# A three-stage kernel on one core: a plan of its own for the first two groups, loads of x ahead of their casts, a second output buffer

## The chip, the core and the metric

The kernel runs on one core of a Trainium2 chip. TensorE (PE) multiplies, VectorE (DVE) and ScalarE (ACT) work on its results, GpSimd (POOL) sets up constants, and the SyncE queue (SP) issues all DMAs. The metric is the device time of one execution, in microseconds; 0.2% is 2.1 us.

## The reference

```python
qn = q / (np.linalg.norm(q, axis=1, keepdims=True) + 1e-06)   # q, k, v: 1 x 6016 x 256
kn = k / (np.linalg.norm(k, axis=1, keepdims=True) + 1e-06)
s = kn.transpose(0, 2, 1) @ qn / tau                          # 256 x 256
a = softmax(s)                                                # rows, with + 1e-09 below
x = v @ a                                                     # 6016 x 256
x = relu(x @ w_in1) ** 2 @ w_out1                             # 256 -> 2048 -> 256
h = x @ w_in2
out = np.maximum(0.01 * h, h) @ w_out2                        # 256 -> 2048 -> 256
```

All in float32; the weights come as 64-bit floats and are turned into 32-bit ones on the chip.

## The kernel before, in words

**Prologue.** The 47 token tiles of q and k come in 14 groups of loads (1, 2, then ten of 4, then 3 and 1 tiles, `groups`). For each group PE adds q^T k into two PSUM banks (L425), ACT squares the group (`square`, L390 to L399), and DVE adds the square to one sum of four tiles (`accumulate`, L406). After the last group DVE folds the sum to one tile (L420 to L422), and eight matmul calls with a vector of ones (`norm_sums`, L373) give the norms. A call in float32 is two instructions in the trace. A chain of small steps follows: norms, scaled product, transposes, exponentials, transposes back (`eT`), and a first **fold** (L277): the attention matrix goes into the first weight block, so that x itself is never formed in the first pass. Between the steps stand matmuls on an identity (`keep_warm`).

**Two passes over units.** Each of the two expert layers is a pass of six panels of tokens by eight groups of 256 hidden columns: 96 units `n` in all, panel by panel. A float32 number is kept as a high and a low part, and every product is three matmuls (`mm3`, L566 to L568: low x high, high x high, high x low). Unit `n` has first products `h` (x with w_in) and second products `y` (g with w_out), the latter issued one or two units later. Units 0 to 7 (`plain`, L684) have four first products of six matmuls, four second products of six, and the fold for the next group; the others (`strassen`, L710) have seven first products of three matmuls. ACT applies relu (L691), square (L662) and the cast to g's high part (L655); DVE makes g's low part (L137). The first products of the plain units take three PSUM banks, a, b, e and a again, each to be freed by its relu.

**Conversions.** A weight block (`Unit`) is turned into high and low parts in some steps of DVE (L173 to L195), a rebias on ACT (L176), a cast on ACT (L222) and a low part on DVE (L137); `whl` is a block of w_in, `wo` one of w_out. For the first pass this runs between the plain units.

**x of later panels** (`prepare_x`). In the first pass v is loaded and transposed; in the second the first pass's result comes back from memory by one DMA into `xr` (L912). ACT casts it in four pieces (L932), DVE makes the lows and three sums.

**Output** (`y_done`, L613 to L627). A finished `y` is copied or transposed from PSUM into the tile `o`, of which there is one, and stored; the very last panel goes another way (`finish_last`, L638 and L639).

**What sets the order.** Nothing is scheduled by need. Each step has a time in a plan (`at`, `on`, `fit`; a unit of the plan is about one matmul of 512 columns), where `fit` looks for a gap in a list of what DVE or ACT already has (`Gaps`). All steps are sorted by these times, and each engine runs its instructions in that order. A plain unit has one table of offsets, stretched by 1.14 (`STRETCH`), 62 units long.

Of the kernel before, what the change touches and what calls it, by code (L numbers as in the profile page):

```python
# [8 lines left out]
F32 = mybir.dt.float32  # L9
# [8 lines left out]
P = 128  # L18
# [32 lines left out]
def attn_moe_moe2(  # L51
# [74 lines left out]

    ts, stt, tt = nc.vector.tensor_scalar, nc.vector.scalar_tensor_tensor, nc.vector.tensor_tensor
    order = tc.manual_schedule()
    order.__enter__()
# [181 lines left out]

    later = []

    def flush():
        while later:
            later.pop(0)()

    def converted(units):

        units[0].exponent()  # L320
        later.append(units[0].rebias)
        yield
        for i, u in enumerate(units):
            if i + 1 < len(units):
                units[i + 1].exponent()
                later.append(units[i + 1].rebias)
                yield
            for step in (u.mantissa, u.mantissa_low, u.sign, u.high):
                step()
                if step == u.high:  # L330
                    later.append(lambda: (u.round(), later.append(u.low)))
                yield
# [8 lines left out]
    with (  # L341
        tc.tile_pool(name="att", bufs=1) as att,
        tc.tile_pool(name="att4", bufs=AHEAD) as att4,
        tc.tile_pool(name="att2", bufs=2) as att2,
    ):
# [21 lines left out]
        steps_o = converted([first_o])  # L367
        W0 = 4

        def norm_sums(src, first):  # L370

            for b in range(4):
                nc.tensor.matmul(  # L373
                    pn[:, b : b + 1],
                    src[:, b * P : (b + 1) * P],
                    ones,
                    start=first and b == 0,
                    stop=not first,
                    skip_group_check=True,
                )  # L380


# [3 lines left out]
        def square(n, t):  # L386
            g = groups[n][1]
            flat = t.rearrange("p g a c -> p g (a c)")
            if n == whole[0]:
                nc.scalar.activation(acc, flat, AF.Square)  # L390
                return
            squares[n] = att2.tile([P, G, 2 * C], F32, tag="sq", name="sq")
            if n < NS - 1:
                nc.scalar.activation(squares[n][:, :g], flat[:, :g], AF.Square)
                return

            last = squares[n][:, 0]
            nc.scalar.activation(last[:, :C], flat[:, 0, :C], AF.Square)
            nc.scalar.activation(ordered(last[:, C:]), in_order(flat[:, 0, C:]), AF.Square)  # L399

        def accumulate(n):
            if n < whole[0]:
                return
            for i, at in ((0, 0), (1, 1)) if n == whole[0] else ((n, 0),):
                sq, g = squares.pop(i), groups[i][1]
                tt(acc[:, at : at + g], acc[:, at : at + g], sq[:, :g], op=ALU.add)  # L406

        for n, (t0, g) in enumerate(groups):
            t = qk.pop(n)
            last_group = n == NS - 1  # L410
            square(n, t)
            if last_group:
                nc.scalar.activation(small[:, 7, 0:1], ones, AF.Sqrt)
            flush()
            if n and not last_group:
                accumulate(n - 1)
            if last_group:
                accumulate(n - 1)
                a0, a1 = acc[:, 0], acc[:, 1]
                tt(acc[:, 0:2], acc[:, 0:2], acc[:, 2:4], op=ALU.add)  # L420
                tt(sums_[:, :C], a0[:, :C], a1[:, :C], op=ALU.add)
                tt(ordered(sums_[:, C:]), in_order(a0[:, C:]), in_order(a1[:, C:]), op=ALU.add)  # L422
# [12 lines left out]
            if W0 <= n < W0 + 4:  # L435
                run(steps_i, 2)
            elif W0 + 4 <= n < W0 + 6:
                run(steps_i, 1)
            if n + AHEAD < NS:
                load_qk(n + AHEAD)  # L440
            elif n + AHEAD == NS:
                load_v(0, 0)
                first_o.load()
                nc.sync.dma_start(tau_sb, tau.partition_broadcast(P))
                load_v(0, 1)
            if n == W0 + 7:
                for u in others[:2]:
                    u.load()
            if last_group:
                norm_sums(squares[n][:, 0], True)  # L450
                norm_sums(sums_, False)
        flush()
        run(steps_o, 2)
        later.pop(0)()
        nc.vector.reciprocal(rtau, tau_sb)
# [16 lines left out]
        run(steps_o, 1)  # L472
        flush()
        s = [bank("e", "s0"), bank("y3", "s1")]
# [30 lines left out]
        x_transpose(1, 0)  # L505
        x_high(0)
        for i in range(KC):
# [8 lines left out]
        for j in range(KC):  # L516
            split(*eT[j], pe[j][:, :C])
        x_high(3)
        x_transpose(0, 1)
# [3 lines left out]
        for i in range(KC):  # L523
            fold_high(i, *first_fold[i])
            fold_low(i, *first_fold[i])
        store_folded(0)
        x_transpose(1, 1)
        x_high(1)
        x_high(2)
        run(steps_o, 3)  # L530
        x_low(1)
        x_low(2)
        flush()
        flush()
        first_o.store()
# [7 lines left out]
    plan = []  # L543
    DVE, ACT = Gaps(), Gaps()

# [13 lines left out]
    LAST = 2 * NP * NG - 1  # L559
    STRETCH = 1.14  # L560
    units = {}
    g_t, c_t, s_t, y_t, h_t = {}, {}, {}, {}, {}

    def mm3(ps, a, b, first, last):
        (ah, al), (bh, bl) = a, b
# [32 lines left out]
    def y_done(t, n, half):  # L598
# [9 lines left out]
        def take(d):  # L608
            ys = y_t[key]
            if d == 0:  # L610
                o[0] = vpool.tile([P, 16, C // Q], F32, tag="o", name="o", bufs=1)
            if L == 2:
# [61 lines left out]
    def plain(n, t0):  # L674

        L, p, g = units[n]
        w = WIDTH[p]
        T = lambda x: t0 + STRETCH * x
        x_at = {(0, 0): (2, 0), (0, 1): (2, 1), (1, 1): (1, 0), (1, 0): (1, 1)}

        def first(half, fb, tag):
            h = h_t[n, half, fb] = bank(tag, "h")
            for kc in range(KC):
                which, at_ = x_at[kc, half]  # L684
                a, b = both(wi_t[L, p, g], 2 * kc + fb), both(x_t[(L, p), which], at_, slice(0, w))
                mm3(h[:, :w], a, b, kc == 0, kc == KC - 1)

# [5 lines left out]
        if g + 1 < NG:  # L693
            pw = {}
            at(T(24), lambda: pw.update(enumerate(fold(g + 1))))
            for i in range(KC):
                on(ACT, T(31 + 2.2 * i), 2.1, lambda i=i: fold_high(i, *pw[i]))
                on(DVE, T(37 + 2.6 * i), 2.5, lambda i=i: fold_low(i, *pw[i]))
            at(T(43), store_folded, g + 1)
        for x, half, fb, tag in ((0, 0, 0, "a"), (12, 0, 1, "b"), (30.4, 1, 0, "e"), (42.4, 1, 1, "a")):  # L700
            at(T(x), first, half, fb, tag)
            on(ACT, T(x + 6.4), 2.7, relu, half, fb)
        for half, x in ((0, 21.2), (1, 51.6)):
            on(ACT, T(x), 4.6, nonlinear, n, half, w, "square")
            on(ACT, T(x + 4.2), 4.6, nonlinear, n, half, w, "cast")
            on(DVE, T(x + 9), 5.4, nonlinear, n, half, w, "low")
        seconds(T, n, ((6, (2, 1, 1)), (18, (1, 0, 0)), (36.4, (1, 0, 1)), (48.4, (1, 1, 0))))

# [88 lines left out]
    for n in range(LAST + 1):  # L797
        L, p, g = units[n] = n // (NP * NG) + 1, n // NG % NP, n % NG
        lengths.append(54.4 * STRETCH if n < NG else 45 * (WIDTH[p] + 32) / 544)
        start.append(now)  # L800
# [56 lines left out]
    for i, u in enumerate(others):  # L857
        end = convert(u, 0, i < 2)
        due = start[u.g - 1] + 24 * STRETCH if u.kind == "i" else start[u.g + 1] + 18 * STRETCH
        assert end < due, (u.kind, u.g, end, due)  # L860
# [32 lines left out]
    def prepare_x(L, p):  # L893
# [108 lines left out]
```

## Time and profile before

| | us |
|---|---|
| median of 3 runs (1073.13 to 1074.63) | 1074.62 |
| the profiled execution | 1073.74 |
| its span, first to last instruction | 1072.0 |
| PE busy in it | 1043.0 |
| DVE busy | 788.6 |
| ACT busy | 716.7 |

The prologue takes the first 62 us of the span, the eight plain units go on to about 164 us, the second pass begins near 570 us. Busy times of engines overlap; what counts is where PE stands still or runs at the lower of its two clocks, and which engine it waits for there.

### The profile page before, as it was taken

What the parts mean: (1) busy time and instruction counts of PE and PEld (TensorE: products, weight loads), DVE (VectorE), ACT (ScalarE), POOL (GpSimd) and SP (SyncE); (2) the same over time, 40 slices, a digit from 0 to 9 for tenths busy, and PEclk for the clock granted to TensorE, in tenths of its full rate; (3) what the DMA queues carried; (4) which work ended last, traced back from release to release, by engine and by line L of the source; (5) the groups of instructions that cost most, each with busy time, mean ns of one, the idle gap of its engine ahead of it and who ended that gap; (6) DMA issues with size and microseconds to landing.
All of it is one profiled execution on the core that took longest, in us unless ns stands there. A gap on an engine that the chain in (4) does not pass through costs nothing.

```text
span 1072.0 us, 12819 instructions
## 1 busy us (share of the span) xinstructions
PE 1043.0 (97%) x4774; PEld 879.4 (82%) x4774; DVE 788.6 (74%) x1097; ACT 716.7 (67%) x851; POOL 0.7 (0%) x6
## 2 busy tenths in 40 slices
PE   8979999999999999999998999999999999999997
PEld 6758888888888788998886888888888888898886
DVE  3899956887988888888885756766766765766554
ACT  5568867888888887887885655655555555555543
POOL 0000000000000000000000000000000000000000
PEclk9989999999999999999998999999999999999999
DMA  9939338557658758656556435535544544645431
GB/s 331 267 136 260 136 99 189 188 223 201 226 210 260 231 195 272 220 222 253 217 211 235 161 119 201 168 142 190 161 160 176 167 162 158 191 162 174 160 119 40
DMA packets 118590, 203.48 MB, mean 190 GB/s; under 512 B 52608, under 2 KB 66176, under 8 KB 116864
## 3 DMA queue, kind: packets, MB, share of 16 engines
q1 hardware_dynamic: 118528, 202.66, 55.9%
q8 instruction: 38, 0.62, 0.2%
q14 instruction: 24, 0.20, 0.1%
HBM read 165.15 MB, written 37.49 MB: 189 GB/s over the span
## 4 chain that ended last, share of the span: by engine, by line
PE 87%; DMA 5%; DVE 4%; SPq 1%; ACT 1%; issue 1%; DVEq 0%
PE y L568 14%; PE y L566 14%; PE y L567 14%; PE hc L566 4%; PE hc L568 3%; PE hc L567 3%; PE ha L566 3%; PE ha L567 3%; PE ha L568 3%; PE hb L566 3%; PE hb L568 3%; PE hb L567 3%; PE sT L425 2%; DMA xr<-x 2%; PE y L586 2%; PE he L566 2%
## 5 line engine op out<-in xcount | busy, mean ns | idle before, releaser
L567 PE MATMUL y<-g,wo 128*128 128x512 f32 (+1 forms) x736 | 283.9, 386 | 0.0
L566 PE MATMUL y<-g,wo 128*128 128x512 f32 (+1 forms) x736 | 283.8, 386 | 0.0
L568 PE MATMUL y<-g,wo 128*128 128x512 f32 (+1 forms) x736 | 283.8, 386 | 0.0
L137 DVE TENSOR_TENSOR g<-c,g 128x1024 fp32r<-128x1024 f32 (+1 forms) x192 | 230.4, 1200 | 30.3 <-ACT g L655 24.5
L655 ACT CAST g<-c 128x1024 fp32r<-128x1024 f32 (+1 forms) x192 | 198.8, 1035 | 4.6
L664 ACT ACTIVATE c<-c 128x1024 f32<-128x1024 f32 (+1 forms) x96 | 100.3, 1045 | 139.4 <-DVE c L754 139.0
L567 PEld LDWEIGHTS y<-g,wo 128*128 128x128 f32 x736 | 138.5, 188 | 26.1
L568 PEld LDWEIGHTS y<-g,wo 128*128 128x128 f32 x736 | 138.5, 188 | 25.9
L566 PEld LDWEIGHTS y<-g,wo 128*128 128x128 f32 x736 | 138.5, 188 | 25.7
L660 ACT ACTIVATE c<-c 128x1024 f32<-128x1024 f32 (+1 forms) x80 | 83.2, 1040 | 41.4 <-DVE c L754 41.1
L754 DVE TENSOR_TENSOR c<-u,hc 128x512 f32<-128x512 f32 (+1 forms) x88 | 59.5, 676 | 58.6 <-PE hc L568 57.7
L662 ACT ACTIVATE c<-c 128x1024 f32<-128x1024 f32 (+1 forms) x96 | 100.4, 1045 | 1.8
L754 DVE TENSOR_TENSOR c<-c,hb 128x512 f32<-128x512 f32 (+1 forms) x88 | 59.3, 674 | 57.2 <-PE hb L568 51.9
L754 DVE TENSOR_TENSOR c<-w,hc 128x512 f32<-128x512 f32 (+1 forms) x88 | 59.2, 672 | 40.5 <-PE hc L568 39.8
L743 ACT COPY u<-ha 128x512 f32<-128x512 f32 (+1 forms) x88 | 50.9, 578 | 56.5 <-PE ha L568 54.1
L754 DVE TENSOR_TENSOR w<-u,he 128x512 f32<-128x512 f32 (+1 forms) x88 | 59.2, 673 | 33.2 <-PE he L568 31.2
L566 PE MATMUL hc<-x,wi 128*128 128x512 f32 (+1 forms) x176 | 69.1, 393 | 6.8 <-DVE c L754 6.8
L567 PE MATMUL ha<-x,wi 128*128 128x512 f32 (+1 forms) x176 | 68.1, 387 | 0.0
L566 PE MATMUL hb<-x,wi 128*128 128x512 f32 (+1 forms) x176 | 68.1, 387 | 0.0
L566 PE MATMUL ha<-x,wi 128*128 128x512 f32 (+1 forms) x176 | 68.1, 387 | 0.0
L567 PE MATMUL hc<-x,wi 128*128 128x512 f32 (+1 forms) x176 | 68.0, 387 | 0.0
L568 PE MATMUL hc<-x,wi 128*128 128x512 f32 (+1 forms) x176 | 68.0, 386 | 0.0
(122 smaller groups left out, 1515.2 us busy)
## 6 DMA issues: line engine op xcount, KB each, us to landing
wi<-wi SPq DMA_DIRECT2D x80, 896.0 KB, 4.9
wo<-wo SPq DMA_DIRECT2D x96, 512.0 KB, 5.6
wi<-wi SPq DMA_DIRECT2D x24, 512.0 KB, 3.6
wst<-in_moe_w_in_dram SPq DMA_DIRECT2D x16, 512.0 KB, 5.6
wst<-in_moe_w_out_dram SPq DMA_DIRECT2D x16, 512.0 KB, 4.4
wi<-wis SPq DMA_DIRECT2D x8, 1024.0 KB, 4.8
qk<-in_q_dram SPq DMA_DIRECT2D x10, 512.0 KB, 8.2
qk<-in_k_dram SPq DMA_DIRECT2D x10, 512.0 KB, 8.3
```

The source lines that it names most:

```text
L137: tt(lo, x, raw(hi), op=ALU.subtract)
L425: nc.tensor.matmul(sT[j][:, :C], t[:, i, 0, j * P : (j + 1) * P], t[:, i, 1], start=n == 0 and i == g - 1, stop=last_group and i == 0,)
L566: nc.tensor.matmul(ps, al, bh, start=first, stop=False, skip_group_check=True)
L567: nc.tensor.matmul(ps, ah, bh, start=False, stop=False, skip_group_check=True)
L568: nc.tensor.matmul(ps, ah, bl, start=False, stop=last, skip_group_check=True)
L586: nc.tensor.matmul(ys[t // 2][:, t % 2 * C : (t % 2 + 1) * C], gt[:, a, fb, t * P : (t + 1) * P], wo[:, b, :, fb], start=first and m == 0 ...
L655: nc.scalar.copy(g_t[n, half][:, 0, :, :w], c)
L660: nc.scalar.activation(c, c, AF.Relu)
L662: nc.scalar.activation(c, c, AF.Square)
L664: nc.scalar.activation(c, c, AF.Prelu, alpha=0.01)
L743: nc.scalar.copy(to, h_t[n, tag][:, :w])
L754: tt(to, x, h_t[n, tag][:, :w], op=ALU.add)
```

## The change

- *Norms.* DVE sums only the ten groups of four; the squares of the last two groups (3 tiles and 1) go straight to the norm products, which are 16 calls instead of 8. There are three square buffers instead of two. Conversions start one group later, and a pending step of ACT now comes ahead of the group's square, one of DVE behind its accumulation.
- *After the exponentials* one cast of x moves behind the casts of `eT`, and both highs of the first folded block come ahead of both lows.
- *Plain units.* Units 0, 1 and the rest have a table each (`PLAIN`), 36, 50 and 62 units long; unit 1 has its four first products in a row, ahead of the fold and of unit 0's second products. The first products take banks a, b, e in turn over all units. Their three matmuls are high x high, high x low, low x high.
- *x in the second pass.* The load keeps its time in the plan; the first step on it comes 66 units later instead of 22.
- *Output.* In the second pass `o` takes its buffer from the pool of v's tiles, which has two.

```diff
-            if n < NS - 1:
+            if n <= whole[-1]:
                 nc.scalar.activation(squares[n][:, :g], flat[:, :g], AF.Square)
                 return
...
+            nc.scalar.activation(squares[n][:, :g, :C], flat[:, :g, :C], AF.Square)
+            for i in range(g):
+                nc.scalar.activation(ordered(squares[n][:, i, C:]), in_order(flat[:, i, C:]), AF.Square)
...
-            if last_group:
-                norm_sums(squares[n][:, 0], True)
-                norm_sums(sums_, False)
+        for i in range(3):
+            norm_sums(squares[NS - 2][:, i], first=i == 0)
+        norm_sums(sums_)
+        norm_sums(squares[NS - 1][:, 0], last=True)
...
+    PLAIN = [
+        dict(first=(0, 6, 18.4, 24.4), fold=12, second=(), length=36, relu=(6.4, 12.4, 26.9, 34.2), stretch=1,
+             square=(18, 36.9), cast=(29.6, 44.4), low=(34.7, 49.5), fold_high=22.6, fold_low=27),
...
-        nc.tensor.matmul(ps, al, bh, start=first, stop=False, skip_group_check=True)
-        nc.tensor.matmul(ps, ah, bh, start=False, stop=False, skip_group_check=True)
-        nc.tensor.matmul(ps, ah, bl, start=False, stop=last, skip_group_check=True)
+    def mm3(ps, a, b, first, last, terms=((1, 0), (0, 0), (0, 1))):
+        for i, (m, n) in enumerate(terms):
+            nc.tensor.matmul(ps, a[m], b[n], start=first and i == 0, stop=last and i == 2, skip_group_check=True)
...
+                o[0] = vpool.tile([P, 16, C // Q], F32, name="o", **({"tag": "v"} if L == 2 else {"tag": "o", "bufs": 1}))
...
-        ot = vpool.tile([P, G, C], F32, tag="o", name="o", bufs=1)
+        ot = vpool.tile([P, G, C], F32, tag="v", name="o")
...
-            begin += LOAD
+            begin += 3 * LOAD
```

On PE, from unit 1's first products on, before (`h` first products, `y` second products, `pw` the fold):

```order
L566 MATMUL h<-x_402,wi 128x512
L567 MATMUL h<-x_402,wi 128x512
L568 MATMUL h<-x_402,wi 128x512
L566 MATMUL h<-x_403,wi 128x512
L567 MATMUL h<-x_403,wi 128x512
L568 MATMUL h<-x_403,wi 128x512
L566 MATMUL y_640<-g,wo 128x512
L567 MATMUL y_640<-g,wo 128x512
L568 MATMUL y_640<-g,wo 128x512
L566 MATMUL y_641<-g,wo 128x512
L567 MATMUL y_641<-g,wo 128x512
L568 MATMUL y_641<-g,wo 128x512
```

And now:

```order
L574 MATMUL h<-x_416,wi 128x512 x3
L574 MATMUL h<-x_417,wi 128x512 x3
L574 MATMUL h<-x_416,wi 128x512 x3
L574 MATMUL h<-x_417,wi 128x512 x3
L574 MATMUL h<-x_416,wi 128x512 x3
L574 MATMUL h<-x_417,wi 128x512 x3
L574 MATMUL h<-x_416,wi 128x512 x3
L574 MATMUL h<-x_417,wi 128x512 x3
L278 MATMUL pw<-whl,eT 128x256 x12
L574 MATMUL y_662<-g,wo 128x512 x3
L574 MATMUL y_663<-g,wo 128x512 x3
L574 MATMUL y_662<-g,wo 128x512 x3
```

Before, a second product of unit 0 stands after two first products of unit 1 (the second of them is shown); now unit 1's four first products and the fold stand ahead of three second products, the first and half of the second of which are shown.

On ACT, from the first relu (`c<-h`) on, before:

```order
L691 ACTIVATE c<-h 128x512
L222 CAST whl<-cm 128x512
L176 ACTIVATE ce<-ce,rebias 128x512
L691 ACTIVATE c<-h 128x512
L662 ACTIVATE c<-c 128x1024
L655 CAST g<-c 128x1024
L295 ACTIVATE wi<-pw,rs 128x256 x2
L691 ACTIVATE c<-h 128x512
L222 CAST wo<-cm 128x512
L176 ACTIVATE ce<-ce,rebias 128x512
L691 ACTIVATE c<-h 128x512
L662 ACTIVATE c<-c 128x1024
```

And now:

```order
L700 ACTIVATE c<-h 128x512 x2
L223 CAST whl<-cm 128x512
L669 ACTIVATE c<-c 128x1024
L296 ACTIVATE wi<-pw,rs 128x256 x2
L700 ACTIVATE c<-h 128x512
L662 CAST g<-c 128x1024
L700 ACTIVATE c<-h 128x512
L669 ACTIVATE c<-c 128x1024
L700 ACTIVATE c<-h 128x512
L662 CAST g<-c 128x1024
L700 ACTIVATE c<-h 128x512
L669 ACTIVATE c<-c 128x1024
```

Of the four conversion steps (the casts of `whl` and `wo`, two rebiases `ce`) that stood between the first four relus, the cast of `whl` is left; the highs of the fold (`wi<-pw`) come ahead of the first cast to `g`, which now stands behind the third relu.

On ACT, where the second panel of the second pass is prepared (`x<-xr` the casts of the loaded panel), before:

```order
L662 ACTIVATE c<-c 128x1024
L655 CAST g<-c 128x1024
L743 COPY u<-ha 128x512
L222 CAST wos<-cm 128x512
L932 CAST x_4925<-xr 128x512
L664 ACTIVATE c<-c 128x1024
L655 CAST g<-c 128x1024
L618 COPY o<-y_4305 128x512
L664 ACTIVATE c<-c 128x1024
```

And now:

```order
L752 COPY u<-ha 128x512
L223 CAST wis<-wr 128x1024
L223 CAST wos<-cm 128x512
L671 ACTIVATE c<-c 128x1024
L662 CAST g<-c 128x1024
L625 COPY o<-y_4319 128x512
L671 ACTIVATE c<-c 128x1024
L752 COPY c<-ha 128x512
L662 CAST g<-c 128x1024
L625 COPY o<-y_4357 128x512
L752 COPY u<-ha 128x512
L943 CAST x_5023<-xr 128x512
```

The first cast of the loaded panel, of 512 columns, has moved from ahead of the leaky relu (the ACTIVATE `c<-c` after it) to behind the next group's copy of `u`, one unit later.

## Rows read from the trace of the kernel before

**Rows 1.** The page's first part: busy us, share of the span, instructions.
```profile
PE 1043.0 (97%) x4774; PEld 879.4 (82%) x4774; DVE 788.6 (74%) x1097; ACT 716.7 (67%) x851; POOL 0.7 (0%) x6
```

**Rows 2.** Busy time by stretch: length, engines' busy us, PE's granted clock, DMA.
```profile
core 0: us, PE busy (x) PEld busy (x) DVE busy (x) ACT busy (x) POOL busy (x), PEclk, DMA share, GB/s
10.10:48.20 38.10, 38.10 (x176) 33.29 (x176) 28.66 (x23) 22.89 (x15) 0.00 (x0) 1.00 1.13 331
...
50.40:57.10 6.70, 5.17 (x23) 4.87 (x24) 4.93 (x15) 2.97 (x6) 0.00 (x0) 0.50 0.19 69
...
70.80:76.90 6.10, 0.00 (x0) 0.00 (x0) 5.96 (x11) 6.04 (x11) 0.00 (x0) 0.78 0.65 218
...
84.00:94.00 10.00, 10.00 (x48) 8.38 (x48) 9.86 (x18) 8.54 (x13) 0.00 (x0) 1.00 1.20 281
...
576.00:582.80 6.80, 5.58 (x13) 4.41 (x14) 3.59 (x5) 3.45 (x5) 0.00 (x0) 0.50 0.26 84
```

**Rows 3.** Timeline of PE from 48 to 95: start, us, instruction, idle before.
```profile
48.77 1.05 PE L373 MATMUL pn<-ones,sq 128*128 128x1 f32 x8 [0.48 <-ACT sq L398]
...
51.90 1.87 PE L373 MATMUL pn<-ones,sums 128*128 128x1 f32 x8 [2.08 <-DVE sums L421]
...
59.57 1.89 PE L277 MATMUL pw<-whl,eT 128*128 128x256 f32 x12
...
62.75 0.50 PE L566 MATMUL h<-x,wi 128*128 128x512 f32 x1 [1.29 <-DVE wi L298]
...
77.00 0.79 PE L566 MATMUL h<-x,wi 128*128 128x512 f32 x1 [6.26 <-ACT c L691]
...
90.02 0.39 PE L566 MATMUL h<-x,wi 128*128 128x512 f32 x1
...
94.10 0.39 PE L566 MATMUL y<-g,wo 128*128 128x512 f32 x1
```

**Rows 4.** Groups of instructions, 62 to 104: busy us, mean ns, idle before.
```profile
L691 ACT ACTIVATE c<-h 128x512 f32<-128x512 f32 x13 | 7.7, 595 | 3.4 <-PE h L568 3.4
L195 DVE SCALAR_TENSOR_TENSOR cm<-cm,ce 128x512 f32<-128x512 f32 x10 | 6.9, 692 | 0.3
L662 ACT ACTIVATE c<-c 128x1024 f32<-128x1024 f32 x6 | 6.4, 1062 | 0.2
L137 DVE TENSOR_TENSOR g<-c,g 128x1024 fp32r<-128x1024 f32 x5 | 6.1, 1218 | 0.0
...
L295 ACT ACTIVATE wi<-pw,rs 128x256 fp32r<-128x256 f32 x7 | 3.0, 474 | 0.8 <-DVE wi L298 0.8
```

**Rows 5.** The chain that ended last, in order of time: start, us, what.
```profile
80.78 0.42 PE h L568
81.20 0.23 PE h L566
...
482.40 7.39 DMA xr<-x
...
566.17 9.03 DMA xr<-x
```

**Rows 6.** Timeline of PE at the four later waits.
```profile
491.81 0.50 PE L566 MATMUL hc<-x,wi 128*128 128x512 f32 x1 [1.01 <-DVE c L754]
...
577.22 0.79 PE L566 MATMUL hc<-x,wi 128*128 128x512 f32 x1 [3.76 <-DVE c L754]
...
836.53 0.50 PE L566 MATMUL hc<-x,wi 128*128 128x512 f32 x1 [0.45 <-DVE c L754]
...
918.37 0.47 PE L566 MATMUL hc<-x,wi 128*128 128x448 f32 x1 [1.05 <-DVE c L754]
```

**Rows 7.** Timeline of the end, all engines.
```profile
1061.46 3.03 PE L586 MATMUL y<-wo,g 128*128 128x256 f32 x24
...
1067.01 0.76 DVE L638 COPY o<-y 128x256 f32<-128x256 f32 x2 [4.63 <-DMA out_dram<-o]
...
1068.20 0.40 SPq L639 DMA_DIRECT2D out_dram<-o  x1
```

More of the change, by code (lines that the diff above doesn't have):

```diff
@@ L127, in attn_moe_moe2 @@
     ts, stt, tt = nc.vector.tensor_scalar, nc.vector.scalar_tensor_tensor, nc.vector.tensor_tensor
+    DVE, ACT = Gaps(), Gaps()
     order = tc.manual_schedule()
@@ L310, in x_tile, with flush @@
         return x_t[key, which]
[L312 to L316, printed above, removed]
+    later = {ACT: [], DVE: []}
+    def flush(engine):
+        steps, later[engine] = later[engine], []
+        for step in steps:
+            step()
     def converted(units):
         units[0].exponent()
-        later.append(units[0].rebias)
+        later[ACT].append(units[0].rebias)
         yield
@@ L325, in converted @@
                 units[i + 1].exponent()
-                later.append(units[i + 1].rebias)
+                later[ACT].append(units[i + 1].rebias)
                 yield
@@ L330, in converted @@
                 if step == u.high:
-                    later.append(lambda: (u.round(), later.append(u.low)))
+                    later[ACT].append(u.round)
+                    later[ACT].append(lambda u=u: later[DVE].append(u.low))
                 yield
@@ L367, in attn_moe_moe2, with norm_sums @@
         steps_o = converted([first_o])
-        W0 = 4
-        def norm_sums(src, first):
+        W0 = 5
+        def norm_sums(src, first=False, last=False):
             for b in range(4):
+                x = src[:, b * P : (b + 1) * P]
                 nc.tensor.matmul(
[L374 to L379, printed above, removed]
+                    pn[:, b : b + 1], x, ones, start=first and b == 0, stop=last, skip_group_check=True
                 )
@@ L410, in attn_moe_moe2 @@
             last_group = n == NS - 1
+            flush(ACT)
             square(n, t)
@@ L413, in attn_moe_moe2 @@
                 nc.scalar.activation(small[:, 7, 0:1], ones, AF.Sqrt)
-            flush()
-            if n and not last_group:
-                accumulate(n - 1)
-            if last_group:
[L418 to L422, printed above, removed]
+            accumulate(n - 1)
+            flush(DVE)
             for i in reversed(range(g)):
@@ L524, in attn_moe_moe2 @@
             fold_high(i, *first_fold[i])
+        for i in range(KC):
             fold_low(i, *first_fold[i])
@@ L529, in attn_moe_moe2 @@
         x_high(2)
-        run(steps_o, 3)
         x_low(1)
         x_low(2)
-        flush()
-        flush()
+        run(steps_o, 3)
+        flush(ACT)
+        flush(DVE)
         first_o.store()
@@ L694, in plain @@
             pw = {}
-            at(T(24), lambda: pw.update(enumerate(fold(g + 1))))
+            at(T(m["fold"]), lambda: pw.update(enumerate(fold(g + 1))))
             for i in range(KC):
[L697 to L707, printed above, removed]
+                on(ACT, T(m["fold_high"] + 2.2 * i), 2.1, lambda i=i: fold_high(i, *pw[i]))
+                on(DVE, T(m["fold_low"] + 2.6 * i), 2.5, lambda i=i: fold_low(i, *pw[i]))
+            at(T(m["fold_low"] + 6), store_folded, g + 1)
+        for i, (half, fb) in enumerate(((0, 0), (0, 1), (1, 0), (1, 1))):
+            at(T(m["first"][i]), first, half, fb, "abe"[(4 * n + i) % 3])
+            on(ACT, T(m["relu"][i]), 2.7, relu, half, fb)
+        for half in range(2):
+            on(ACT, T(m["square"][half]), 4.6, nonlinear, n, half, w, "square")
+            on(ACT, T(m["cast"][half]), 4.6, nonlinear, n, half, w, "cast")
+            on(DVE, T(m["low"][half]), 5.4, nonlinear, n, half, w, "low")
+        seconds(T, n, m["second"])
     def strassen(n, t0):
@@ L858, in attn_moe_moe2 @@
         end = convert(u, 0, i < 2)
-        due = start[u.g - 1] + 24 * STRETCH if u.kind == "i" else start[u.g + 1] + 18 * STRETCH
+        n, x = (u.g - 1, "fold") if u.kind == "i" else (u.g + 1, "second")
+        m = PLAIN[min(n, 2)]
+        due = start[n] + m["stretch"] * (m[x] if u.kind == "i" else 18)
         assert end < due, (u.kind, u.g, end, due)
```

38 lines of the change are left out of this document (20 added, 18 removed).

## Prediction

> **What bounds the kernel now.** I read the page's first part, then the busy time and granted clock by stretch, then the timeline of the stretches that fall short, and last the chain that ended last. TensorE (PE) is busy 1043.0 of 1072.0 us [rows 1]; the other engines matter only where they make PE wait. By stretch [rows 2] the products of q and k keep PE busy for all of 10.1 to 48.2 at a granted clock of 1.00 (2.4 GHz), so an earlier square moves nothing there. From 50.4 to 57.1 the clock is 0.50 (1.2 GHz). From 70.8 to 76.9 PE does nothing while VectorE (DVE) is busy 5.96 of 6.1 us and ScalarE (ACT) 6.04. From 84 to 94 PE is full again, with DVE at 9.86 of 10. The timeline names the wait: the product at 77.00 stood 6.26 us for an ACT relu [rows 3]. Later PE waits at 491.81, 577.22, 836.53 and 918.37 [rows 6], and after PE's last product there is a tail of stores [rows 7]. Everything else is PE at one 128x512 matmul in 0.23 us [rows 5], which the change leaves alone: it removes no large matmul.
>
> **The change, part by part.**
>
> *Norms.* Gone are one accumulation of 1536 columns and DVE's place on the path; added are eight calls of one column on PE (16 calls instead of 8, two instructions each). In the trace eight such instructions take 1.05 us early and 1.87 us once the clock is 0.50 [rows 3]. PE is free at 48.3 as before, and squares and sums should be ready by then: DVE has one accumulation less, and ACT no longer waits for a square buffer. The 32 instructions take 4.2 us at the first rate (end 52.5) and, if the clock falls at about 50.4 as it does now, some 16 at the first and 16 at the second, 5.8 us (end 54.1). Before, the last one ended at 51.90 + 1.87 = 53.8. So -1.3 to +0.3 us; the cast of x that no longer stands ahead of ACT's eT casts gives 0 to 0.3 more. I take **-0.3** for both, nearer the second end, because the same kind of work stands there when the clock falls now.
>
> *The first two groups.* Before, the fold starts at 59.57 and the first product at 62.75 [rows 3]. I follow the new order from a fold that ends at 61.3, with durations from [rows 4]; a step of 128x512 without a row of its own is priced as its nearest there, 0.69 on DVE and 0.60 on ACT. ACT writes both highs (0.47 each) by 62.2, then DVE both lows by 63.2; the first product now asks for highs first, so it starts near 61.9 and ends at 63.7 (six matmuls, 1.4 us); the second ends at 65.1, the fold for group 1 at 66.5, the third at 67.9. DVE meanwhile transposes x, makes two lows of x, and sign and high of wo: 66.6. ACT casts wo, DVE makes its low and the next exponent, ACT rebiases that, and only then comes the first relu (0.60): 69.4. So PE waits about 1.5 us before product four, which ends at 70.8. The fold's highs come after the second relu, the whl cast and a square (1.06): 72.7, the lows 73.7. Product one of group 1 waits 1.5 us for the first high and 0.4 for the low, and ends at 74.2. From there three banks taken in turn are enough: relus end at 73.3, 74.9 and 76.5, each before its bank is wanted. Products end at 78.4, the fold at 79.8, three second products (18 matmuls, 4.1 us) at 83.9, with g's lows (1.22 each) long done. Group 2 begins there; before, it began at 90.02 [rows 3]. DVE then owes g's low, the high of wo, two steps of the next unit and wo's low, ready at about 89.0, while PE wants it at 88.0: a wait of 1 us. The same product stood at 94.10 [rows 3]: **-5.1 us**. Bounds: -8.4 if no wait is left (6.3 us of idle time, and ten matmuls at 0.42 instead of 0.23 us [rows 3, 5]); 0 if DVE, full to 9.86 of 10 [rows 2], gives nothing. I take the worked value, being the one with its queue counted. From group 3 on my count finds DVE ahead of PE (two conversions of some 3.6 us, two lows of g and two of the fold, 10.6 us of DVE in the 12.4 us that 48 matmuls and a fold take on PE), so the gain stays.
>
> *x begun sooner.* In the second pass the plan now leaves 66 instead of 22 units between the load and the first cast of x. The order shows the load where it was on SP and the cast about one group later on ACT, 10 us. Before, loads issued at 482.40 and 566.17 take 7.39 and 9.03 us [rows 5], ACT stands in order behind the cast, and PE waits 1.01 and 3.76 us [rows 6]. A cast 10 us later (at about 579 for the worse one, against a landing at 575.2) finds its data. The second wait also took the clock: 13 matmuls in 576 to 582.8 at 0.50 [rows 2], 0.2 us too much each, 2.6 us. Together **-7.4 us**. Nothing on PE asks for x before the next group of eight, some 30 us later.
>
> *Two output buffers.* At 836.53 and 918.37 PE waits 0.45 and 1.05 us [rows 6] behind transposes into the one output tile that is still being stored; with a second tile those go: -1.5. At the end PE's last 24 matmuls start at 1061.46 and are done at about 1064.4, but DVE's copy waits 4.63 us for a store and starts at 1067.01, and the last store is issued at 1068.20 [rows 7]. Now the copies start with PE's results: four of about 0.4 us, of which ACT's wait for DVE's, from 63.9 to 65.4, and the store 2.8 us sooner. **-4.3 us** in all, the surest term. What is late next is PE's end itself.
>
> *Later conversions and stores* change places on SP, DVE and ACT but not in number; PE has no wait on a weight's DMA in the whole trace, and I cost them at 0 (1 us if one store holds up a load).
>
> *Sum*: 0.3 + 5.1 + 7.4 + 4.3 = 17.1 us off the profiled execution's 1073.74 (1072.0 of span and 1.7 around it): **1056.6 us**. That execution lies 0.9 us under the median of 1074.62, and I add nothing for it.
>
> **The clock, where the order makes short gaps.** By [rows 2, 3] the clock fell after PE had stood idle 6.3 us, after 3.76, and in the prologue after 2 us of idle time beside one-column matmuls; it did not after waits of 1.0 us [rows 6]. My count puts waits of 1.5 and 1.9 us close together at 68 to 74, between those cases. On the side of a fall stands the Trainium skill ("TensorE: Matmul & The Clock Gate", section "A second HAM failure mode: psum-queue depth-cycling"): a kernel that cycles through PSUM banks idles PE briefly between groups often enough that the clock swings between its two levels. The trace shows no such swing for the waits of 1 us; for two of 1.5 it has no row.
>
> **The rivals.**
> 1. *The clock falls again at about 74.* As after 576, some 14 matmuls then run 0.2 us slower, up to 3.4 us over such a stretch; the wait of 1 us for wo takes up 0.9 of that. 2.5 us lost: 1059.1 us. For it: two gaps close together. Against it: each is shorter than the ones that did it, and PE works between them.
> 2. *The x casts only move the wait.* The later casts leave the lows and sums of x less room before the next eight groups. If one comes late, the wait and the slow stretch stand at the end of the preparation: the 7.4 us are not had, 1064.0 us. Against it: DVE's 74% of the span [rows 1] holds the crowded early groups, so it has room here.
> 3. *The second buffer does not decouple*, because the tile shares its slots with v's: the 4.3 us stay, 1060.9 us. Against it: v's last tile is read before the second pass.
> 4. *Slower: DVE becomes the bound of groups 2 to 7.* If the wait of 1 us for wo comes back in each of the six groups, and each is followed by a slow stretch as at 577.22 (2.6 us), that is 6 x 3.6 = 21.6 us against 17.1 gained: 1078.2 us. It decides from 17.1 / 6 = 2.85 us a group, so with slow stretches of 2.6 us a wait of 0.25 us each time is enough. For it: DVE at 9.86 of 10 [rows 2]. Against it: waits of 1 us took no clock so far.
>
> **How the numbers follow.** Forecast (1055 to 1058.5) 0.55; clock falls 0.25; x only moves 0.08; buffers 0.05; slower 0.05; the rest, 0.02, is better than the forecast by more than 2 us, with the prologue at 2.4 GHz and no wait early (down to 1052). Leaving out the slower case, most of the moved x and that rest gives a range of 1053.0 to 1062.0. This kernel's runs can tell 0.2% from no change, about 2.1 us. All cases but the fourth are faster by more than that: faster 0.93, the same 0.03 (a partial fourth case), slower 0.04.
>
> **What would show it.** Right: group 2's first product near 84, clock 1.00 from there to the end with no half-speed stretch at 576; no wait of PE over 0.5 us after 480 on casts of x or stores; the last store issued about 1.1 us after PE's end instead of 3.8. Wrong: a granted clock of 0.50 between 70 and 90 (rival 1), ACT still waiting on the load of x (rival 2), the last copy waiting on a store (rival 3), or PE waiting on DVE in every one of groups 2 to 7 (rival 4).

## The result, and the profile after

| | before | changed |
|---|---|---|
| median, us (same chip) | 1074.53 (4 runs, 1073.13 to 1074.63) | 1064.08 (4 runs, 1062.22 to 1065.53) |
| the profiled execution | 1073.74 | 1062.22 |
| its span | 1072.0 | 1060.3 |

The ratio is 0.9905, 95% interval 0.9887 to 0.9922. The change is faster, by 10.5 us of the 18 that were forecast: 1056.6 was predicted, with a range from 1053.0 to 1062.0, so the range doesn't hold the time.

The page's first part of the changed kernel, as [rows 1]:

```profile
PE 1042.3 (98%) x4798; PEld 881.1 (83%) x4798; DVE 786.8 (74%) x1096; ACT 715.8 (68%) x854; POOL 0.7 (0%) x6
```

PE does the same work, 24 instructions more; what was gained is standing still and slow stretches. By stretch, with the columns of [rows 2]:

```profile
50.40:57.10 6.70, 6.67 (x36) 6.38 (x36) 2.16 (x9) 2.11 (x4) 0.00 (x0) 0.58 0.01 3
...
70.80:76.90 6.10, 4.44 (x19) 3.02 (x18) 5.76 (x11) 5.61 (x9) 0.00 (x0) 1.00 0.70 241
...
576.00:582.80 6.80, 3.39 (x15) 2.53 (x14) 2.90 (x5) 3.05 (x5) 0.00 (x0) 1.00 0.56 218
584.00:587.40 3.40, 3.40 (x9) 2.67 (x8) 1.35 (x2) 1.92 (x4) 0.00 (x0) 0.50 0.67 229
```

Between 70.8 and 76.9 PE now works for 4.44 us, where it did nothing before. In the prologue it is busy for 6.67 of 6.70 us, and the granted clock is still 0.58. At the first panel of the second pass PE stands for half of a stretch, and then runs at 0.50 for 3.4 us. The timeline of PE at the start answers to [rows 3]:

```profile
52.23 1.85 PE L377 MATMUL pn<-ones,sq 128*128 128x1 f32 x8
...
62.56 0.73 PE L574 MATMUL h<-x,wi 128*128 128x512 f32 x2 [0.56 <-ACT wi L296]
...
70.12 1.66 PE L574 MATMUL h<-x,wi 128*128 128x512 f32 x6 [1.29 <-ACT c L700]
73.25 0.73 PE L574 MATMUL h<-x,wi 128*128 128x512 f32 x2 [1.46 <-ACT wi L296]
74.18 5.29 PE L574 MATMUL h<-x,wi 128*128 128x512 f32 x22 [0.19 <-DVE wi L299]
...
84.84 1.52 PE L574 MATMUL h<-x,wi 128*128 128x512 f32 x6
...
88.93 1.53 PE L574 MATMUL y<-g,wo 128*128 128x512 f32 x6
```

The one wait of 6.26 us has become three of 1.29, 1.46 and 0.19 us, and group 2 starts at 84.84 instead of 90.02.

To see where the rest went, one can follow one kind of instruction through both traces. ACT's squares and leaky relus come in the same order in both:

| the instruction starts at | before | changed | lead so far |
|---|---|---|---|
| 7th (first groups over) | 107.27 | 102.11 | 5.2 |
| 91st (end of the first pass) | 541.84 | 537.27 | 4.6 |
| 103rd (second pass begun) | 608.49 | 602.36 | 6.1 |
| 169th (after PE's last wait of before) | 943.84 | 934.90 | 8.9 |
| end of the span | 1072.0 | 1060.3 | 11.7 |

From the second row to the third 6.4 of the 7.4 us of the later casts of x had been expected (3.76 us of waiting and 2.6 of a slow stretch), and 1.6 were had; the other 1.0, at 491, falls between the first two rows, where nothing was gained. The timeline of that place, ACT, SP, DVE and PE of the changed kernel in order of time (`o<-y` is the copy of a finished product into the output tile, `x<-o` its store, `x<-xr` a cast of the loaded panel):

```profile
568.83 0.57 ACT L625 COPY o<-y 128x512 f32<-128x512 f32 x1
...
570.79 1.74 SPq L634 DMA_DIRECT2D x<-o  x2
...
578.69 0.59 ACT L625 COPY o<-y 128x512 f32<-128x512 f32 x1 [5.48 <-DMA x<-o]
579.17 0.59 ACT L752 COPY u<-ha 128x512 f32<-128x512 f32 x1
...
579.65 0.63 ACT L943 CAST x<-xr 128x512 fp32r<-128x512 f32 x1
579.80 0.69 DVE L763 TENSOR_TENSOR w<-u,he 128x512 f32<-128x512 f32 x1 [5.33 <-ACT u L752]
...
582.52 0.96 PE L574 MATMUL hc<-x,wi 128*128 128x512 f32 x3 [3.41 <-DVE c L763]
583.33 2.19 PE L574 MATMUL y<-g,wo 128*128 128x512 f32 x6
```

The cast of x no longer waits for anything, as predicted. But the copy ahead of it does: the first pass ends with two halves of a panel, its output tile is single, and the second half's copy waits 5.48 us for the first half's store. Behind that copy stands `u`, behind `u` DVE's `w`, behind it PE's product: a wait of 3.41 us, and six matmuls that take 2.19 instead of 1.52. The chain of waits has the store itself in it, here and one panel earlier:

```profile
489.54 6.21 DMA x<-o
...
572.10 6.49 DMA x<-o
```

All waits of that kind on ACT in the view of waits (total us, times, longest), of the changed kernel:

```profile
ACT o L625 <- DMA x<-o: 15.6, 5, 5.5
```

And of the kernel before, two rows that the prediction didn't use:

```profile
ACT x L932 <- DMA xr<-x: 14.6, 5, 5.4
ACT o L618 <- DMA x<-o: 11.4, 5, 2.8
```

The waits for the load (14.6 us) are gone, those for the store were there all along, and have grown. The two copies at the same place of the kernel before:

```profile
577.78 0.58 ACT L618 COPY o<-y 128x512 f32<-128x512 f32 x1
...
586.42 0.59 ACT L618 COPY o<-y 128x512 f32<-128x512 f32 x1 [2.14 <-DMA x<-o]
```

There too the second copy waited for the first half's store, but PE did not stand for it: it had come out of its slow stretch at 582.8 and still had work.

At the end, as [rows 7]:

```profile
1052.54 3.03 PE L592 MATMUL y<-wo,g 128*128 128x256 f32 x24
...
1054.89 0.42 DVE L645 COPY o<-y 128x256 f32<-128x256 f32 x1 [1.44 <-PE y L592]
...
1056.47 0.39 SPq L646 DMA_DIRECT2D out_dram<-o  x1
```

The copies wait for PE alone, and the last store is issued 0.9 us after PE's end (3.7 before).

### The profile page after: what moved, and what is told of

It reads as the page before. It is cut to its first block, busy times and chain, and to the rows that moved or that the text cites. A ratio compares the mean times of both kernels' runs of the same rounds, so it can differ in the third digit from the quotient of the medians.

```text
span 1060.3 us, 12864 instructions
## 1 busy us (share of the span) xinstructions
PE 1042.3 (98%) x4798; PEld 881.1 (83%) x4798; DVE 786.8 (74%) x1096; ACT 715.8 (68%) x854; POOL 0.7 (0%) x6
## 4 chain that ended last, share of the span: by engine, by line
PE 92%; DMA 3%; DVE 2%; issue 1%; SPq 1%; ACT 1%; DVEq 0%; ACTq 0%
PE y L574 43%; PE hc L574 11%; PE ha L574 10%; PE hb L574 10%; PE he L574 5%; PE sT L423 4%; PE h L574 4%; PE y L592 2%; DMA v<-in_v_dram 1%; DMA x<-o 1%; PE pw L278 1%; DVE c L763 1%; PE pn L377 1%; PE warm L135 0%; DMA wst<-in_moe_w_in_dram 0%
## 5 line engine op out<-in xcount | busy, mean ns | idle before, releaser
L574 PE MATMUL y<-g,wo 128*128 128x512 f32 (+1 forms) x2208 | 551.6, 385 | 0.0
L574 PE MATMUL hc<-x,wi 128*128 128x512 f32 (+1 forms) x528 | 146.7, 386 | 5.0 <-DVE c L763 4.9
L574 PE MATMUL hb<-x,wi 128*128 128x512 f32 (+1 forms) x528 | 146.6, 386 | 0.3 <-DVE c L763 0.3
L574 PEld LDWEIGHTS hc<-x,wi 128*128 128x128 f32 x528 | 98.6, 188 | 25.1 <-DVE c L763 7.2
L574 PEld LDWEIGHTS hb<-x,wi 128*128 128x128 f32 x528 | 99.5, 189 | 19.3 <-DVE c L763 0.8
L574 PEld LDWEIGHTS ha<-x,wi 128*128 128x128 f32 x528 | 98.8, 189 | 17.6
L574 PE MATMUL he<-x,wi 128*128 128x512 f32 (+1 forms) x264 | 73.0, 385 | 0.0
L763 DVE TENSOR_TENSOR c<-w,hb 128x512 f32<-128x512 f32 (+1 forms) x88 | 59.4, 675 | 9.5 <-DVE w L763 0.5
L752 ACT COPY c<-ha 128x512 f32<-128x512 f32 (+1 forms) x88 | 50.8, 577 | 20.3 <-PE ha L574 19.9
L574 PEld LDWEIGHTS he<-x,wi 128*128 128x128 f32 x264 | 49.6, 188 | 9.3
```

The costliest lines, as they stand in the source:

```text
L574: nc.tensor.matmul(ps, a[m], b[n], start=first and i == 0, stop=last and i == 2, skip_group_check=True)
L752: nc.scalar.copy(to, h_t[n, tag][:, :w])
L763: tt(to, x, h_t[n, tag][:, :w], op=ALU.add)
```

## The experiments

My theory (A) was that the single output tile of the first pass holds PE at 497 and 582; the rival (B), that the transfers or the order around the panel's end do so, whatever the tile.

**1. Three half tiles.** In place of a second whole tile (4 KB a partition), the tile is cut in two halves and a third half is added:

```diff
-                o[0] = vpool.tile([P, 16, C // Q], F32, name="o", **({"tag": "v"} if L == 2 else {"tag": "o", "bufs": 1}))
+            if d == 0 and L == 2:
+                o[0] = vpool.tile([P, 16, C // Q], F32, tag="v", name="o")
...
-            to = o[0].rearrange("p g c -> p (g c)")[:, d * w : (d + 1) * w]
+            o[d] = vpool.tile([P, 512], F32, tag="o", name="o", bufs=3)
+            to = o[d][:, :w]
```

> The changed kernel with the first pass's output tile cut into halves of 128x512, three of them in turn instead of two that go together. Theory A (what holds PE at 497.11 and 582.52 in the changed kernel is ACT's copy into the one output tile, whose store is still under way): the wait of 1.14 us at 497 goes, of the 3.57 us at 582.52 at most 1 us is left (DVE's second copy still waits for the first half's store), and the eight matmuls at half clock (1.6 us) go: 5.3 to 6.4 us off the changed kernel's 1064.1, 1058.2 us. Theory B (the transfers or DVE's own order around the panel's end hold PE, and the copy only shows it first): PE waits 2 to 4 us at the same product on something else, 1062 to 1064 us.

Measured: 1058.22 us, ratio 0.9843 (0.9826 to 0.9860). The timeline of the same place (DVE's copy of the second half, and PE's product):

```profile
575.00 0.59 ACT L625 COPY o<-y 128x512 f32<-128x512 f32 x1
...
579.87 0.69 DVE L625 COPY o<-y 128x512 f32<-128x512 f32 x1 [1.35 <-DMA x<-o]
...
581.21 0.96 PE L574 MATMUL hc<-x,wi 128*128 128x512 f32 x3 [0.20 <-DVE c L762]
```

ACT's copy waits for nothing; DVE's waits 1.35 us for the first half's store; PE waits 0.20, and no slow stretch follows. Theory A is shown: with another place to put the result, the wait and the stretch go.

**2. The later cast alone**, in the kernel before: `begin += LOAD` becomes `begin += 3 * LOAD`.

> The kernel before with one edit: the first cast of x in the second pass comes 66 instead of 22 units behind its load. Theory A (the copy into the one output tile binds a little behind the cast): the waits move from 491.81 and 577.22 to the next group, ACT stands for the store, and 1 to 2 us are gained, near 1073. Theory B (the cast's wait for the load was the only one there, and the first groups' new plan brought the other): 7.4 us gained, 1067.1.

Measured: 1073.51 us, ratio 0.9985 (0.9972 to 0.9999). On ACT, and PE behind it:

```profile
585.72 0.58 ACT L618 COPY o<-y 128x512 f32<-128x512 f32 x1 [5.42 <-DMA x<-o]
```

```profile
589.55 0.79 PE L566 MATMUL hc<-x,wi 128*128 128x512 f32 x1 [3.35 <-DVE c L754]
```

Theory A: the wait stands behind the copy into the output tile also without the rest of the change, so the first groups' new plan did not bring it.

**3. Three halves, cast of x early** (experiment 1 with `begin += LOAD`).

> The changed kernel with the three halves, but the first cast of x back at 22 units behind its load. Theory A (two waits stand close together, and either alone holds PE): the casts wait for the load again as before the change (1.0 and 3.8 us, and a slow stretch of 2.6), so it is within 1.5 us of the changed kernel, 1065. Theory B (only the output tile ever bound): as good as with the later casts, 1058.

Measured: 1063.62 us, ratio 0.9894 (0.9875 to 0.9913), in six runs from 1060.35 to 1066.23; the profiled one is the slowest. ACT, and PE behind it:

```profile
571.75 0.62 ACT L942 CAST x<-xr 128x512 fp32r<-128x512 f32 x1 [3.68 <-DMA xr<-x]
```

```profile
573.75 1.20 PE L574 MATMUL hc<-x,wi 128*128 128x512 f32 x3 [2.06 <-DVE c L762]
574.75 2.77 PE L574 MATMUL y<-g,wo 128*128 128x512 f32 x6
```

The wait for the load is back, and with it six matmuls at 2.77 us. Either wait alone holds PE.

**4. The fourth corner**: the changed kernel with `begin += LOAD`, beside the changed kernel itself on the same chip.

> The changed kernel with the first cast of x in the second pass back at 22 units behind its load, and still one output tile in the first pass. Theory A (of the two waits that stand close together the later cast takes away one only): 1 to 2 us slower than the changed kernel, 1065.6. Theory B (the later cast did bring a good part of what the prediction asked of it, and the output tile only limits the rest): 4 us or more slower, 1068 or above.

> The changed kernel itself, once more, as the reference for the other three on their chip: 1064.1, within 1 us.

Measured: 1066.26 (0.9919, 0.9904 to 0.9934) and 1063.75 us (0.9901, 0.9886 to 0.9917). ACT, one cast and one copy that wait; on PE two waits in place of one:

```profile
572.18 0.62 ACT L943 CAST x<-xr 128x512 fp32r<-128x512 f32 x1 [3.64 <-DMA xr<-x]
...
582.60 0.59 ACT L625 COPY o<-y 128x512 f32<-128x512 f32 x1 [3.83 <-DMA x<-o]
```

```profile
574.17 0.96 PE L574 MATMUL hc<-x,wi 128*128 128x512 f32 x3 [2.02 <-DVE c L763]
...
586.44 0.96 PE L574 MATMUL hc<-x,wi 128*128 128x512 f32 x3 [1.77 <-DVE c L763]
```

The later cast is worth 2.5 us by the medians, a little more than expected (the intervals overlap), less than theory B's 4. The four corners together:

| | cast early | cast late |
|---|---|---|
| one output tile in the first pass | 1066.26 | 1063.75 |
| three halves | 1063.62 | 1058.22 |

Each edit by itself gives some 2.5 us by the medians, both 8.0. The two rows come from two chips, on which the kernel before took 1074.73 and 1074.97 us, and with the spread of experiment 3 the 2.6 us of the halves alone are the least sure of these. With both waits in place PE stood 2.02 and 1.77 us, and neither was followed by a slow stretch. With the load's wait gone, the store's grew to 3.41 us; with the store's gone, the load's stayed at 2.06; a slow stretch followed each. The early cast also costs something later: PE waits 1.26 us at 741.25 (1.54 at 740.88 in experiment 3), and with the later cast it does not.

**5. The buffers of the second pass alone**, in the kernel before (tag `v` for `o` in the second pass and in `finish_last`).

> The kernel before with one edit: the second pass's output tile and the last one take their buffer from the pool of v's tiles, which has two. If the waits of the second pass behind output stores and the tail are independent of the other parts: 2.8 us less between 590 and 920 and 2.8 less after PE's last product, 1068.9. If the prediction's own sizes hold: 4.3 less, 1070.2. If the tile does not decouple without the other parts: no change, 1074.5.

Measured: 1069.85 us, ratio 0.9956 (0.9939 to 0.9973). At the end, DVE's copy and the last store:

```profile
1060.34 0.42 DVE L638 COPY o<-y 128x256 f32<-128x256 f32 x1 [1.44 <-PE y L586]
...
1061.91 0.40 SPq L639 DMA_DIRECT2D out_dram<-o  x1
```

The buffers work without the other parts. The time lies between the two sizes (1068.9 and 1070.2), and its interval holds both, so the trace has to tell the size. From the 103rd to the 169th instruction of the table it takes 333.4 us for 335.3 before: 1.9 less, with 0.74 and 1.33 had at the two waits of [rows 6] at 836 and 918. From the 169th to the end it is 2.7 less. That makes 4.6 us for the buffers; the changed kernel has 2.8 in the first of these stretches, and the other 0.9 belong to the later cast of x, as experiment 2's trace gains 0.7 at the three panel starts near 661, 743 and 825, and this one nothing there. This execution was also 2.5 us shorter from the 91st to the 103rd instruction: PE stood 2.21 and 1.54 us there, with no slow stretch, where before it stood 3.76 and had one. No run shows that the buffers did that.

**6. The old plan back** in experiment 1's kernel: `m = PLAIN[2]` for all plain units, and their length.

> The kernel with three halves, with the old table of offsets for all eight plain units (62 units long each); banks, order of the three matmuls and prologue stay as changed. Theory A (the gain of the first groups comes from the table): PE waits some 5 us for a relu again before the fourth first product of unit 0 or in unit 1, the stretch at half clock behind it is back, and 5.2 us are lost against the kernel with three halves (1058.2): 1063.4. Theory B (the banks in turn and the moved conversions bring most of it): at most 2.5 us lost, 1060.5.

Measured: 1062.82 us, ratio 0.9887 (0.9873 to 0.9901), 4.6 us more than with the new plan. PE in the first groups:

```profile
76.29 0.74 PE L574 MATMUL h<-x,wi 128*128 128x512 f32 x2 [3.79 <-ACT wi L296]
77.97 4.63 PE L574 MATMUL h<-x,wi 128*128 128x512 f32 x10 [0.94 <-DVE wi L299]
```

The gain comes from the table, theory A. The wait is not the relu's this time but that for the fold's high, and ten matmuls take 4.63 us.

**7. The old prologue back** in experiment 1's kernel.

> The kernel with three halves, with the prologue as before the change (norms from one sum of all tiles, conversions one group earlier, a cast of x ahead of those of eT, each high followed by its low). Theory A (the new norms are worth next to nothing): the first product after the fold starts within 0.5 us of where it did, measured from the last product of q and k, and the time is within 1 us of 1058.2. Theory B (the longer row of one-column products costs what it adds at half clock): 1 us or more is gained by going back, 1057.

Measured: 1056.61 us, ratio 0.9832 (0.9817 to 0.9847); against experiment 1's 0.9843 that is not told apart by the times. From the first norm product to the first product of unit 0 it is 62.69 - 49.21 = 13.5 us in this execution, in the changed kernel 62.56 - 48.39 = 14.2. The other profiles don't settle it. From the end of the last product of q and k to the first product of unit 0, the old prologue takes 13.3 us here, 13.8 in experiment 5, 14.5 in the kernel before and 15.1 in experiment 2; the new one with one column takes 14.0 to 14.2 in six profiles and 15.6 in one. So the new norms are worth next to nothing, and it is not shown which prologue is the faster.

**8. Wider ones**: the norm products with 64 equal columns of ones in place of one.

```diff
-                    pn[:, b : b + 1], x, ones, start=first and b == 0, stop=last, skip_group_check=True
+                    pn[:, 64 * b : 64 * b + 64], x, wide, start=first and b == 0, stop=last, skip_group_check=True
```

> The kernel with three halves, with 64 equal columns of ones in place of one in the norm products (same count of instructions; the norms are read from every 64th column). Theory A (the clock falls at 51.5 because PE's work there is one column wide, though it never stands still): it stays at 1.00 to 58, the last eight norm instructions take about 1.0 instead of 1.85 us and the small products behind them run at full rate: 1.3 to 2 us off, 1056.6. Theory B (the clock falls there whatever the width, or the wider ones cost what it gives): no gain, 1058.2 to 1059.

Measured: 1057.19 us, ratio 0.9832 (0.9814 to 0.9850). The last eight instructions on PE, and the stretch behind:

```profile
52.04 1.06 PE L380 MATMUL pn<-wide,sq 128*128 128x64 f32 x8
```

```profile
52.00:57.00 5.00, 4.00 (x35) 3.72 (x35) 3.25 (x13) 2.65 (x6) 0.00 (x0) 1.00 0.03 11
```

The clock stays at 1.00, eight instructions of 64 columns cost 1.06 us (one column: 1.85 at the falling clock), and the first product comes 61.07 - 48.52 = 12.6 us after the first norm product instead of 14.2. By the trace theory A; the time alone (1 us, intervals that overlap) would not show it. In all eleven profiles with one column the clock falls between 50.3 and 55.9; in this one and the two below that also have 64 columns it is at 1.00 all that time.

**9. Relus first.** Experiment 1's kernel, with the cast of `wo` behind the first relu, and group 1's fold highs and lows moved ahead of the square.

> The kernel with three halves, with the cast of wo behind the first relu instead of ahead of both, and the highs and lows of group 1's fold ahead of the first square and the low of whl. Theory A (PE's waits of 1.3, 1.5 and 0.2 us at 70.12, 73.25 and 74.18 are only the order on ACT): two thirds or more go, 2 to 2.7 us off, 1055.9. Theory B (DVE, busy 5.76 of 6.1 us there, has no room and the wait comes back at the next fold or at wo): under 0.7 us, 1057.8.

Measured: 1057.51 us, ratio 0.9834 (0.9819 to 0.9849). ACT, and PE behind it:

```profile
71.24 0.62 ACT L223 CAST whl<-cm 128x512 fp32r<-128x512 f32 x1 [0.86 <-DVE cm L196]
...
71.77 0.83 ACT L296 ACTIVATE wi<-pw,rs 128x256 fp32r<-128x256 f32 x2
...
72.29 4.95 PE L578 MATMUL h<-x,wi 128*128 128x512 f32 x13 [1.97 <-ACT wi L296]
```

My expectation failed: from the first product to the 7th instruction it takes 39.7 us, as in experiment 1 (39.6). The relu's wait went, but the highs still stood behind the cast of `whl`, which waits for DVE, and one wait of 1.97 us with a slow stretch took the place of two without.

**10. Old prologue, kept warm**: experiment 7's kernel with the wide ones, `keep_warm(warm, 6)` between the two norm products and `keep_warm(warm, 7)` for 4 ahead of the transposes.

> The kernel with three halves and the prologue as before, and in it six more identity matmul calls where PE waits for DVE's sums, three more ahead of the transposes, and norms from 64 equal columns of ones. With the prologue as before it was 1056.6. Theory A (the steps behind the norms run at half clock only because PE stood for 1.7 us and then did one-column work): clock 1.00 to 60, the first product 0.9 to 1.5 us sooner, 1055.4. Theory B (the clock falls there anyway, or the added calls are in the way): 1056.6 to 1057.5.

Measured: 1055.27 us, ratio 0.9818 (0.9801 to 0.9834). The stretch behind the norms, which has 0.52 (53 to 60) in experiment 7:

```profile
52.00:60.00 8.00, 7.41 (x59) 6.59 (x58) 7.08 (x25) 5.61 (x13) 0.00 (x0) 1.00 0.02 4
```

Theory A: the first product comes 12.3 us after the first norm product, 13.5 in experiment 7. Which share the wider ones have in it and which the added matmuls is not told apart.

**11. Relus and highs**, on experiment 10's kernel: in `PLAIN[0]` the first relus at 3 and 10.5, and for unit 0 the highs at 13 and the lows at 14, ahead of the cast of `whl`.

> The kernel of the run before this one, with both first relus of unit 0 ahead of the rebiases and group 1's fold highs and lows ahead of the cast of whl, for which the earlier try had left them waiting. Theory A (the waits at the first products are the order on ACT, and only that cast spoiled the earlier try): 1.5 to 2.2 us less than the run before, 1053.5. Theory B (DVE has no room): within 0.5 us of it, 1055.2.

Measured: **1052.64 us**, ratio 0.9793 (0.9777 to 0.9810), the fastest here: 22 us under before, 11 under the changed kernel. ACT's highs, and PE's longest wait behind the first product:

```profile
68.11 0.83 ACT L296 ACTIVATE wi<-pw,rs 128x256 fp32r<-128x256 f32 x2
```

```profile
70.14 1.19 PE L581 MATMUL h<-x,wi 128*128 128x512 f32 x4 [0.68 <-DVE wi L299]
```

Theory A, and DVE had room: from the first product to the 7th instruction it takes 37.5 us, 40.4 in experiment 10. Some of that belongs to a slow stretch at 72 in the profile of experiment 10, of the kind below.

**The clock in the first groups.** The changed kernel's second profile (the reference of experiment 4) shows what its first does not. PE, and the stretches:

```profile
73.59 0.73 PE L574 MATMUL h<-x,wi 128*128 128x512 f32 x2 [1.46 <-ACT wi L296]
74.51 3.68 PE L574 MATMUL h<-x,wi 128*128 128x512 f32 x8 [0.18 <-DVE wi L299]
```

```profile
70.50:74.50 4.00, 2.37 (x8) 1.32 (x8) 3.87 (x9) 3.30 (x7) 0.00 (x0) 1.00 0.92 294
74.50:78.00 3.50, 3.49 (x8) 2.80 (x9) 2.51 (x4) 3.47 (x5) 0.00 (x0) 0.51 0.59 185
```

With the same waits (1.27, 1.46 and 0.18 us) the clock is 0.51 for 3.5 us in this execution, and was 1.00 in the other. The 7th instruction starts 1.9 us later; 0.35 of that stood before the first product (62.91 for 62.56), so the slow stretch cost 1.5. Waits like these are also in the profiles of experiments 1, 3 and 8 and of the first kernel of experiment 4, where the clock stayed at 1.00.

## Why the prediction was right and wrong

*Prologue* (-0.3): -0.2, the first product at 62.56 for 62.75. The norms end at 54.08, at the slow bound (54.1): the last eight instructions take 1.85 us, as the clock falls though PE does not stand still. That the end of the norms sets the first product's time is not shown. In the second profile of the changed kernel the clock falls later, the last eight take 1.03 us and end at 53.10, and the first product still comes 14.3 us after the first norm product (14.2).

*First two groups* (-5.1): right in size; the lead is 5.2 us after them, and the same product of `wo` stands at 88.93, worked out as 89.0. That it agrees so closely is luck, as two errors cancel: group 2 starts 0.9 us later than the worked 83.9, and the wait of 1 us for `wo` did not come. Rival 4 fell with it: no wait of PE over 0.2 us from 75 to 260. The bound of -8.4 is 8.2 by its own terms (6.3 us, and ten times 0.19); nothing else hangs on it.

*x begun sooner* (-7.4): **this step failed**. It took away the wait for the load and counted no wait behind it. It brought 2.3 us in the profile: none of the 1.0 at 491, where PE now stands 0.98 us at 497.11 for the same kind of copy, 1.6 of the 6.4 at 577, and 0.7 that had not been counted, at the panel starts near 661, 743 and 825. Between medians it is 2.5 (experiment 4). "A cast 10 us later finds its data" was right. What was left out is the sentence that follows from it: ACT runs in order, and between the old place of the cast and the new one stands the copy into the single output tile, which waits 5.48 us for a store, and PE 3.41 behind it. I asked what is late next on PE, not on ACT, though the wait for `x<-o` was in the view of waits with 11.4 us. In the kernel before, the slow stretch covered it, the very stretch whose 2.6 us were booked as gain: with PE at half its clock, ACT came to the second copy 6.5 us after the first had begun (577.78, and 586.42 less the wait of 2.14). In the changed kernel it comes 4.4 us after it (568.83, and 578.69 less 5.48). Experiment 5's kernel has the old cast, and no slow stretch there: its second copy is reached after 4.0 us, waits 3.62, and PE stands 1.54. That the stretch covered the wait is read from these traces; no run tests it by itself.

This is rival 2 in its effect, but not in its mechanism: neither lows nor sums of x are late. That the median (1064.08) falls on that rival's 1064.0 is chance, as it is made of other parts. The term itself was the right size for the place once the store's wait is gone too: from the 91st to the 103rd instruction experiment 1 takes 60.3 us for 66.7 before, 6.3 less, of 6.4 worked out.

*Two output buffers* (-4.3): right in kind, 0.6 us too small: 2.8 us in the tail as worked out, and 2.1 instead of 1.5 in the second pass. The two waits cost 0.75 and 1.33 us, more than the idle time that their rows show (0.45 and 1.05): the matmul at 918.37 starts 1.42 us after the one ahead of it, and the one behind it 0.31 us later, where 0.20 is usual there.

*Later conversions and stores* (0, 1 us if held up): 0.6 us lost between the first groups and the end of the first pass, in waits such as 0.33 us at 346.06.

Of the profiled execution, 5.6 us are missed: 5.1 by x, 0.8 by small waits, prologue and first groups, 0.2 by what lies around the span, less 0.6 by the buffers. The median lies another 1.9 us higher, as that execution was the fastest of its four. *Rival 1*, priced at 2.5 us, may be part of why: the clock falls at 74 in one of the two profiles of the changed kernel and not in the other, and the one where it does loses 1.5 us by it. The Trainium skill ("TensorE: Matmul & The Clock Gate", section "A second HAM failure mode: psum-queue depth-cycling"), which the prediction weighed, says of another kernel that cycles through PSUM banks that its brief idle times between groups of products make the clock swing. The second profile agrees, with 0.51 for 3.5 us, and the first does not.

The prediction set the falls of the clock beside whole waits of 6.3, 3.76 and 2 us. The clock stood at 0.50 before these waits were over, from 74.5, 576.0 and 50.4 on, so a wait need not be as long as the first two for it to fall; experiments 3 and 9 have falls with waits of 2.06 and 1.97 us.

## What to carry to other kernels

When a wait on an in-order engine is taken away, read that engine's next instructions for waits that the first one, or a slow stretch behind it, covered, and look for them in the view of waits: their totals stand there also when they cost nothing yet. Two waits close together can be worth less one by one than together: here some 2.5 us each alone, and 8.0 both. A buffer that is single on one side of a change (here the output tile of the first pass) should be looked for on the other side too.

## What the runs showed of the hardware

- In the changed kernel's first profile the clock fell while PE was busy 6.67 of 6.70 us, with products of one column; with 64 columns, the same count of instructions and nearly the same price at full clock (1.06 against 1.03 us for eight) it stayed at 1.00 (experiment 8).
- Waits of about the same length went both ways. After 2.02 and 1.77 us with full work between them (experiment 4's first kernel), and after 2.21 and 1.54 (experiment 5), the clock stayed at 1.00; with 2.06 (experiment 3) and with 1.97 at 72 (experiment 9) it fell; 1.27 and 1.46 us did it in one execution of the changed kernel and not in the other.
- Two stores late in the first pass take 6.2 and 6.5 us in the chain, against medians of 4.5 and 4.7 us from issue to landing over the stores of their sizes (224 and 256 KB).
